# A chunked-attention and feed-forward kernel: ranked copies and splits, weight loads one pair ahead, row turns one group later, residual rows in tiles of their own

## The chip, the cores and the metric

The kernel runs on one core of a Trainium2 chip. A core has TensorE (PE in the profile, with its weight loads as PEld), VectorE (DVE), ScalarE (ACT), GpSimd (POOL) and SyncE (SP, which here only issues DMAs). Each engine works through its own queue in order. The metric is the time of one execution on the device in microseconds (us).

## The reference

Three steps follow one another, all in float32 (weights come as 64-bit numbers). B = 8, H = 8, S = 576, D = 64, so there are 4608 tokens of width 512.

```python
# 1. attention inside chunks of 64 tokens
scores = scale * q_c @ k_c^T                      # per head and chunk, 64x64
attn = softmax(scores); x = attn @ v_c            # -> [8, 576, 512]
# 2. gated mixing
gate = sigmoid(causal depthwise conv of x with conv_w, 5 taps)
x = (gate * (x @ w_val)) @ w_out
# 3. feed-forward with a residual
xn = (x - mean) / sqrt(var + 1e-6) * g_ln
out = x + relu(xn @ w_ch1) @ w_ch2                # 512 -> 2048 -> 512
```

## The kernel before

Every large product is made from three matmuls of halves: an operand is split into a high half (a rounded copy, made by ScalarE) and a low half (the difference, made by VectorE or GpSimd). High halves are named xh, gh, hh, oh, low ones xl, gl, hl, ol; the halves of a feed-forward weight tile are both named w.

**Attention stage (0 to about 382 us).** The tokens are cut into 36 units of 128. A slot `u` transposes k and q of unit u on TensorE (L177), copies them to kT and qT on ScalarE (L178), then transposes the probabilities `pr` of unit u-2 (L219, copied to pT at L220), multiplies q by k (`sc`, L192) and pr by v (`x`, L250). VectorE takes the maximum `mx`, subtracts it (`ex`), ScalarE takes the exponential (L206), and VectorE sums (`sm`, L208), inverts and scales (`pr`, L211). Transposes of k, q and pr share two PSUM tiles with the tag "t", so a transpose waits until the copy out of the tile two before is done. From x, ScalarE makes a copy xf (L264) and the high half xh (L268), and GpSimd the low half xl (L269).

Four units make a block of 512 tokens; there are nine. For each block VectorE runs the convolution `cg` (L281, 16 instructions; ScalarE makes the first tap at L279), ScalarE takes its sigmoid (L288, which needs a table load, as the next exponential does), TensorE forms the values `psv` in four groups of 12 matmuls (L295), VectorE multiplies them by the gate (`gv`, L309), ScalarE and VectorE split that (gh L312, gl L313), and TensorE multiplies by w_out (`pso`, again L295), which ScalarE copies (`y`, L325) and writes to memory. A table `dense` says which slot gets which of these steps. The weights w_out are decoded from 64-bit (ScalarE L107, VectorE L108 to L110: `da`) and split (`oh` L115, `ol` L116) by `split_w`, in four chunks.

**First feed-forward stage (about 382 to 484 us).** The first 512 tokens go through 16 groups f: `ff1` makes psh (12 matmuls), ScalarE and VectorE its halves hh (L393) and hl (L394), `ff2` uses the group before (`acc`, 12 matmuls, L409). Beside that the weights of later groups are loaded, decoded and split (`next_ff`), and the rows of the next 1024 tokens are read in pairs, normalised (`ln_rows`: statistics on VectorE, the root `r` at L357 and the scaled rows `yr` at L366 on ScalarE) and turned (`turn_rows`: 8 transposes per pair at L374).

**Pair stage (about 484 to 1172 us).** The remaining 4096 tokens run in four rounds (`s`) of 8 pairs (`p`) of column groups through `ff_pair`, which works with sums of weights and of rows. The weight sums are made once, in round 0, by `make_pair`: it reads both decoded tiles of a pair back from memory (`raws`, L439 and L440), adds them on VectorE (L441 to L444), splits the sums (`wc`) and writes them out for later rounds. The staging tag "raw" has two tiles, and a pair takes both. In the last pair of a round `ff2_tile` adds the residual rows and writes the result: the upper four tiles from `yt`, read ahead by `load_yt`, the lower four from rows read at that point by `load_rows` (L343, a staging tag with three tiles).

**What sets the order.** TensorE's instructions stand in the order of the program in slots 0 to 6 and again from the first feed-forward stage on (`manual_schedule`). Everything else is ordered by the tile scheduler, which ranks instructions by their place in the program unless they stand in a `high_priority` block.

Of the kernel before, what the change touches and what calls it, by code (L numbers as in the profile page):

```python
# [19 lines left out]
def tile_chunk_attention_gated_mlp(ctx: ExitStack, tc: tile.TileContext, q, k, v, w_val, conv_w, w_out, g_ln, w1, w2, out):  # L20
    nc = tc.nc
# [107 lines left out]
    def split_w(nm):  # L129
        hs, ls = [], []  # L130
        for c, raw in enumerate(wv[nm]):
            hi = pD1.tile([P, DM], F32R, name=f"{nm}h{c}")
            lo = pD1.tile([P, DM], F32R, name=f"{nm}l{c}")
            split(hi, lo, raw)
            hs.append(hi)
            ls.append(lo)
        wv[nm] = (hs, ls)
# [34 lines left out]
    def transpose_in(u, src, dst, nm):  # L172
# [5 lines left out]
        nc.scalar.activation(out=t, in_=ps, func=ACTF.Copy)  # L178
        dst[u] = t
# [34 lines left out]
    def a4(u):  # L214
# [5 lines left out]
        nc.scalar.activation(out=t, in_=ps, func=ACTF.Copy)  # L220
        pT[u] = t
# [18 lines left out]
    def a5(u):  # L240
# [21 lines left out]
        for lo, hi, sh in segs:  # L262
            dst = xf[j][:, :, lo + sh:hi + sh].rearrange("p (r i) t -> p r i t", r=2)
            nc.scalar.activation(out=dst, in_=x[:, :, :, lo - a:hi - a], func=ACTF.Copy)  # L264
        for lo, hi, sh in segs:
            src = xf[j][:, :, lo + sh:hi + sh]
            dst = xh[j][:, :, lo:hi].rearrange("p (r i) t -> p r i t", r=2)
            nc.scalar.activation(out=dst, in_=x[:, :, :, lo - a:hi - a], func=ACTF.Copy)  # L268
            nc.gpsimd.tensor_tensor(out=xl[j][:, :, lo:hi], in0=src, in1=xh[j][:, :, lo:hi], op=ALU.subtract)  # L269
# [27 lines left out]
    def val(j, f):  # L297
        hs, ls = wv["v"]
# [8 lines left out]
        for lo, hi, sh in ((0, o, 0), (o, BLK, HALO)):  # L307
            if lo < hi:
                nc.vector.tensor_tensor(out=gv[:, lo:hi], in0=ps[:, lo:hi], in1=cg[:, f, lo + sh:hi + sh], op=ALU.mult)  # L309
        a = pD1.tile([P, BLK], F32R, tag=f"gh{f}", name="gh")  # L310
        b = pD1.tile([P, BLK], F32R, tag=f"gl{f}", name="gl")
        nc.scalar.activation(out=a, in_=gv, func=ACTF.Copy)  # L312
        nc.vector.tensor_tensor(out=b, in0=gv, in1=a, op=ALU.subtract)  # L313
        gh[j, f], gl[j, f] = a, b

    def proj(j, t):
        hs, ls = wv["o"]
# [7 lines left out]
        nc.scalar.activation(out=y, in_=ps, func=ACTF.Copy)  # L325
        nc.scalar.dma_start(out=y_dram[j][ts, :], in_=y)
# [99 lines left out]

    def make_pair(p):
# [7 lines left out]
        ra, rb = (stg.tile([P, 4, 2 * P], F32, tag="raw", name="raws") for _ in range(2))  # L435
# [3 lines left out]
        nc.sync.dma_start(out=ra[:, 0:2, :], in_=a_dram[2 * p].rearrange("p (c w) -> p c w", c=2))  # L439
        nc.sync.dma_start(out=ra[:, 2:4, :], in_=a_dram[2 * p + 1].rearrange("p (c w) -> p c w", c=2))  # L440
# [45 lines left out]
    def load_yt(s):  # L486
        for i in range(HB, 2 * HB):
            if i % 2 == 0:
                t = p2["yt"].tile([P, 2, DM], F32, name="yt")
            nc.sync.dma_start(out=t[:, i % 2, :], in_=rows(s, i)[0])  # L490
            yt[i] = t[:, i % 2, :]

    def ff2_tile(s, p, h, i):
# [21 lines left out]
        elif last:  # L515
            y = load_rows(s, i)
            nc.vector.tensor_tensor(out=y, in0=ps, in1=y, op=ALU.add)
            nc.sync.dma_start(out=rows(s, i)[1], in_=y)

    def ff_pair(s, p, fill):  # L520
# [6 lines left out]
        def prod(ps, k, nm, start):  # L527
# [109 lines left out]
    def prep(t):  # L637
        nonlocal xn0, yt0
        if t == 0:
# [11 lines left out]
            turn_rows(ln_rows([yt0[:, i, :] for i in range(HB)]), 0)  # L651
# [26 lines left out]
    at(0, (5, 1), lambda: split_w("o"))  # L678
# [28 lines left out]
    next_ff(NFA + 1)  # L707
    ys = {0: pair_rows(0)}
    for f in range(NF):
        ff1(0, f)  # L710
        if f in (3, 5, 7, 9):
            turn_rows(ys.pop(f - 3), f - 3)
# [7 lines left out]
        if f > 0:  # L720
            next_ff(f + NFA + 1)
        if f == NF - 4:
# [14 lines left out]
    for s in range(NS):  # L737
        for p in range(NPR):
            fill = ff_pair(s, p, fill)
            if p == 0:  # L740
                load_yt(s)
# [32 lines left out]
```

## Time and profile before

| | us |
|---|---|
| three runs | 1177.71, 1178.44 (median), 1179.29 |
| profiled execution | 1179.48 |
| its span, first to last instruction | 1177.7 |
| TensorE busy | 1112.4 (94%) |
| VectorE busy | 731.0 (62%) |
| ScalarE busy | 526.3 (45%) |
| GpSimd busy | 159.8 (14%) |

A busy share is a mean over stages. What is read in the rows below is, for each engine, when an instruction started, how long it took, how long the engine had been idle before it, and which instruction ended that idle time.

### The profile page before, as it was taken

The page shows a single profiled execution, that of the slowest core. Times are in us where ns is not written, and L with a number is a line of the kernel's source. Part 1 is how long each engine was busy: PE and PEld are TensorE (multiplying, and loading weights), DVE is VectorE, ACT ScalarE, POOL GpSimd, SP SyncE. Part 2 cuts the span into 40 slices and gives each one's busy share as a digit, 9 for nine tenths or more (in the row PEclk, how much of TensorE's full clock was granted, in tenths as well). Part 3 has the DMA queues.
Part 4 walks back from the last instruction along what each step waited for, and adds up shares of the span by engine and source line. Part 5 has one row for each costly group of instructions (what it writes and reads, how often), then busy time and mean ns, then how long its engine had stood idle before and what let it go on. Part 6 is the DMA issues. An engine that isn't in the chain of part 4 may idle for free.

```text
span 1177.7 us, 18293 instructions
## 1 busy us (share of the span) xinstructions
PE 1112.4 (94%) x7128; PEld 902.3 (77%) x7128; DVE 731.0 (62%) x1237; ACT 526.3 (45%) x972; POOL 159.8 (14%) x160
## 2 busy tenths in 40 slices
PE   6869999899999799989999999999999999999998
PEld 5747777777777687768888788888788887878876
DVE  6878898998794889644653834435734446433433
ACT  4557677676766665434452323423323323221221
POOL 2231143111210444332220000000000000000000
PEclk8979999999999899999999999999999999999999
DMA  7655676665124563534333543332623332622212
GB/s 185 176 117 130 166 191 170 172 158 128 55 65 151 169 210 105 211 129 143 126 125 108 183 138 108 121 111 72 232 90 123 110 107 90 233 78 89 84 36 80
DMA packets 168860, 155.37 MB, mean 132 GB/s; under 512 B 120622, under 2 KB 128838, under 8 KB 168774
## 3 DMA queue, kind: packets, MB, share of 16 engines
q1 hardware_dynamic: 163590, 144.76, 40.3%
q10 hardware_dynamic: 5184, 9.44, 2.1%
q8 instruction: 56, 0.92, 0.3%
q14 instruction: 30, 0.25, 0.1%
HBM read 116.41 MB, written 37.75 MB: 131 GB/s over the span
## 4 chain that ended last, share of the span: by engine, by line
PE 60%; DVE 27%; ACT 6%; issue 3%; DMA 3%; SPq 1%; POOL 1%; DVEq 0%; ACTq 0%; POOLq 0%
PE acc L507 14%; PE x L533 14%; PE psf L507 13%; PE zy L533 9%; DVE cg L281 8%; PE psv L295 3%; DVE pr L211 2%; PE pso L295 2%; DVE sm L208 2%; DVE da L109 2%; DVE da L110 2%; DVE ex L202 1%; DVE gl L313 1%; DVE mx L199 1%; DVE h L543 1%
## 5 line engine op out<-in xcount | busy, mean ns | idle before, releaser
L551 DVE TENSOR_TENSOR c<-x,c 128x512 f32<-128x512 f32 x96 | 66.2, 689 | 231.6 <-ACT c L547 176.3
L507 PE MATMUL acc<-w,h 128*128 128x512 f32 x768 | 186.4, 392 | 0.0
L507 PE MATMUL psf<-w,h 128*128 128x512 f32 x768 | 186.1, 392 | 0.0
L507 PEld LDWEIGHTS acc<-w,h 128*128 128x128 f32 x768 | 144.8, 189 | 31.4
L507 PEld LDWEIGHTS psf<-w,h 128*128 128x128 f32 x768 | 144.4, 188 | 31.2
L533 PE MATMUL x<-t,wc 128*128 128x512 f32 x576 | 146.9, 391 | 2.2 <-DVE c L551 2.2
L547 ACT ACTIVATE c<-zy 128x512 f32<-128x512 f32 x96 | 57.9, 604 | 193.8 <-PE zy L533 193.7
L533 PEld LDWEIGHTS x<-t,wc 128*128 128x128 f32 x576 | 108.1, 188 | 26.0 <-DVE c L551 3.0
L542 ACT ACTIVATE h<-c 128x512 fp32r<-128x512 f32 x96 | 60.5, 631 | 138.1 <-DVE c L551 137.6
L281 DVE SCALAR_TENSOR_TENSOR cg<-xf,cw,cg 128x516 f32<-128x516 f32 (+1 forms) x176 | 116.3, 707 | 0.8 <-ACT cg L279 0.6
L512 DVE TENSOR_TENSOR yt<-psf,yt 128x512 f32<-128x512 f32 x128 | 88.0, 690 | 23.8 <-PE psf L507 19.8
L533 PE MATMUL zy<-b,wc 128*128 128x512 f32 x384 | 98.9, 393 | 0.0
L533 PEld LDWEIGHTS zy<-b,wc 128*128 128x128 f32 x384 | 71.3, 188 | 14.5
L543 DVE SCALAR_TENSOR_TENSOR h<-c,h 128x512 fp32r<-128x512 f32 x96 | 67.7, 705 | 15.6 <-ACT h L542 15.2
L269 POOL TENSOR_TENSOR xl<-xf,xh 128x512 fp32r<-128x512 f32 (+1 forms) x40 | 50.9, 1276 | 153.4 <-ACT xh L268 153.1
L295 PE MATMUL psv<-xh,vh 128*128 128x512 f32 x144 | 60.9, 423 | 6.5 <-DVE gv L309 6.3
L295 PE MATMUL pso<-oh,gh 128*128 128x512 f32 x144 | 60.4, 419 | 6.1 <-ACT gh L312 6.1
L417 POOL TENSOR_TENSOR wc<-raws,wc 128x256 fp32r<-128x256 f32 x56 | 46.8, 856 | 111.9 <-ACT wc L416 111.7
L116 POOL TENSOR_TENSOR w<-da,w 128x512 fp32r<-128x512 f32 x32 | 46.9, 1474 | 95.9 <-ACT w L115 95.9
L295 PE MATMUL psv<-xl,vh 128*128 128x512 f32 x144 | 58.8, 408 | 0.9 <-POOL xl L269 0.9
L295 PE MATMUL pso<-oh,gl 128*128 128x512 f32 x144 | 58.1, 405 | 0.9 <-DVE gl L313 0.9
L533 PE MATMUL x<-b,wc 128*128 128x512 f32 x192 | 52.6, 410 | 6.6 <-DVE h L543 5.9
(114 smaller groups left out, 1779.1 us busy)
## 6 DMA issues: line engine op xcount, KB each, us to landing
wc<-wc SPq DMA_DIRECT2D x112, 512.0 KB, 3.2
raw<-in_moe_w_ch SPq DMA_DIRECT2D x32, 512.0 KB, 4.8
yr<-yd SPq DMA_DIRECT2D x48, 256.0 KB, 3.1
vr<-in_v SPq DMA_DIRECT2D x144, 64.0 KB, 2.7
yd<-y ACTq DMA_DIRECT2D x36, 256.0 KB, 2.5
kr<-in_k SPq DMA_DIRECT2D x64, 128.0 KB, 2.9
qr<-in_q SPq DMA_DIRECT2D x64, 128.0 KB, 2.9
out<-yt SPq DMA_DIRECT2D x20, 256.0 KB, 3.2
```

What stands on the lines that cost most here:

```text
L116: nc.gpsimd.tensor_tensor(out=lo, in0=a, in1=hi, op=ALU.subtract)
L269: nc.gpsimd.tensor_tensor(out=xl[j][:, :, lo:hi], in0=src, in1=xh[j][:, :, lo:hi], op=ALU.subtract)
L281: nc.vector.scalar_tensor_tensor(out=o, in0=x[:, f, i + lo:i + hi], scalar=cw[:, i * CT + f:i * CT + f + 1], in1=o, op0=ALU.mult, op1=ALU.add,
L295: nc.tensor.matmul(out=ps, lhsT=lt, rhs=rh, start=(i == 0), stop=(i == n - 1))
L417: eng.tensor_tensor(out=lo, in0=a, in1=hi, op=ALU.subtract)
L507: nc.tensor.matmul(out=ps, lhsT=lt, rhs=rh, start=(g == 0 and k == 0 and (first or half)), stop=(g == 1 and k == 2 and (last or half)),)
L512: nc.vector.tensor_tensor(out=yt[i], in0=ps, in1=yt[i], op=ALU.add)
L533: nc.tensor.matmul(out=ps, lhsT=lt, rhs=rh, start=(start and c == 0 and i == 0), stop=(c == 1 and i == 2), skip_group_check=True)
L542: nc.scalar.activation(out=t[:, 0, :], in_=src, func=ACTF.Relu)
L543: nc.vector.scalar_tensor_tensor(out=t[:, 1, :], in0=src, scalar=0.0, in1=t[:, 0, :], op0=ALU.max, op1=ALU.subtract)
L547: nc.scalar.activation(out=t, in_=zy, func=ACTF.Copy)
L551: nc.vector.tensor_tensor(out=t, in0=x, in1=t, op=ALU.add)
```

## The change

Six edits in one diff. Copies and splits in the attention stage (kT, qT, pT, xf, xh, xl, gv, gh, gl, y and its write) and the row statistics of the first block move into `high_priority` blocks. `split_w` takes a range of chunks, and w_out's four chunks are placed in slots 5, 6, 7 and 8 instead of all in slot 5. The weights of group 5 are asked for inside the loop, behind the first pair of rows. `turn_rows` is called in groups 4, 6, 8 and 10 instead of 3, 5, 7 and 9. The loads of `make_pair` become `load_pair`, called one pair ahead. `load_yt` reads the lower four residual tiles too, in the last pair of a round, into the staging tag "raw".

```diff
-    def split_w(nm):
-        hs, ls = [], []
-        for c, raw in enumerate(wv[nm]):
+    def split_w(nm, c0=0, c1=CT):
+        hs, ls = wv.setdefault(nm + "s", ([], []))
+        for c, raw in list(enumerate(wv[nm]))[c0:c1]:
...
-        nc.scalar.activation(out=t, in_=ps, func=ACTF.Copy)
-        dst[u] = t
+        with tc.high_priority():
+            nc.scalar.activation(out=t, in_=ps, func=ACTF.Copy)
+            dst[u] = t
...
-        nc.scalar.activation(out=t, in_=ps, func=ACTF.Copy)
-        pT[u] = t
+        with tc.high_priority():
+            nc.scalar.activation(out=t, in_=ps, func=ACTF.Copy)
+            pT[u] = t
...
-        for lo, hi, sh in segs:
-            dst = xf[j][:, :, lo + sh:hi + sh].rearrange("p (r i) t -> p r i t", r=2)
-            nc.scalar.activation(out=dst, in_=x[:, :, :, lo - a:hi - a], func=ACTF.Copy)
...
+        with tc.high_priority():
+            for lo, hi, sh in segs:
+                dst = xf[j][:, :, lo + sh:hi + sh].rearrange("p (r i) t -> p r i t", r=2)
+                nc.scalar.activation(out=dst, in_=x[:, :, :, lo - a:hi - a], func=ACTF.Copy)
...
+        with tc.high_priority():
+            for lo, hi, sh in ((0, o, 0), (o, BLK, HALO)):
+                if lo < hi:
+                    nc.vector.tensor_tensor(out=gv[:, lo:hi], in0=ps[:, lo:hi], in1=cg[:, f, lo + sh:hi + sh], op=ALU.mult)
+            a = pD1.tile([P, BLK], F32R, tag=f"gh{f}", name="gh")
+            b = pD1.tile([P, BLK], F32R, tag=f"gl{f}", name="gl")
+            nc.scalar.activation(out=a, in_=gv, func=ACTF.Copy)
+            nc.vector.tensor_tensor(out=b, in0=gv, in1=a, op=ALU.subtract)
...
-        nc.scalar.activation(out=y, in_=ps, func=ACTF.Copy)
-        nc.scalar.dma_start(out=y_dram[j][ts, :], in_=y)
+        with tc.high_priority():
+            nc.scalar.activation(out=y, in_=ps, func=ACTF.Copy)
+            nc.scalar.dma_start(out=y_dram[j][ts, :], in_=y)
...
+    raws = {}
+
+    def load_pair(p):
+        ra, rb = (stg.tile([P, 4, 2 * P], F32, tag="raw", name="raws") for _ in range(2))
+        for f in range(2):
+            nc.sync.dma_start(out=ra[:, 2 * f:2 * f + 2, :], in_=a_dram[2 * p + f].rearrange("p (c w) -> p c w", c=2))
+        raws[p] = ra, rb
...
-        ra, rb = (stg.tile([P, 4, 2 * P], F32, tag="raw", name="raws") for _ in range(2))
+        ra, rb = raws.pop(p)
...
-    def load_yt(s):
-        for i in range(HB, 2 * HB):
+    def load_yt(s, half):
+        for i in range(half * HB, (half + 1) * HB):
             if i % 2 == 0:
-                t = p2["yt"].tile([P, 2, DM], F32, name="yt")
+                t = p2["yt"].tile([P, 2, DM], F32, name="yt") if half else stg.tile([P, 2, DM], F32, tag="raw", name="yt")
...
-            y = load_rows(s, i)
+            y = yt[i]
...
                 make_pair(p + 1)
+                if p + 2 < NPR:
+                    load_pair(p + 2)
...
-            turn_rows(ln_rows([yt0[:, i, :] for i in range(HB)]), 0)
+            with tc.high_priority():
+                ln_rows([yt0[:, i, :] for i in range(HB)])
+            turn_rows([yt0[:, i, :] for i in range(HB)], 0)
...
-    at(0, (5, 1), lambda: split_w("o"))
+    for c in range(CT):
+        at(0, (5 + c, 1), lambda c=c: split_w("o", c, c + 1))
...
-    next_ff(NFA + 1)
     ys = {0: pair_rows(0)}
     for f in range(NF):
         ff1(0, f)
-        if f in (3, 5, 7, 9):
-            turn_rows(ys.pop(f - 3), f - 3)
+        if f in (4, 6, 8, 10):
+            turn_rows(ys.pop(f - 4), f - 4)
...
-        if f > 0:
-            next_ff(f + NFA + 1)
+        next_ff(f + NFA + 1)
...
+    load_pair(0)
     make_pair(0)
+    load_pair(1)
...
             if p == 0:
-                load_yt(s)
+                load_yt(s, 1)
+            if p == NPR - 1:
+                load_yt(s, 0)
```

What that does to the queues is shown at three places. The first is ScalarE's queue around the sigmoid of block 0 (oh is a split chunk of w_out, ex an exponential, ACT_TABLE_LOAD and the cg behind it the sigmoid). Before:

```order
L178 ACTIVATE kT<-pst 128x512
L115 ACTIVATE oh_762<-da 128x512
L178 ACTIVATE qT<-pst 128x512
L220 ACTIVATE pT<-pst 128x512
L115 ACTIVATE oh_771<-da 128x512
L264 ACTIVATE xf<-x 128x4x128
L268 ACTIVATE xh<-x 128x4x128
L206 ACTIVATE ex_144<-ex_144 128x8x64
L288 ACT_TABLE_LOAD
L288 ACTIVATE cg<-cg 128x4x512
L178 ACTIVATE kT<-pst 128x512
L178 ACTIVATE qT<-pst 128x512
```

And with the change:

```order
L178 ACTIVATE kT<-pst 128x512
L290 ACT_TABLE_LOAD
L290 ACTIVATE cg<-cg 128x4x512
L178 ACTIVATE qT<-pst 128x512
L221 ACTIVATE pT<-pst 128x512
L115 ACTIVATE oh_859<-da 128x512
L315 ACTIVATE gh<-gv 128x512 x2
L115 ACTIVATE oh_991<-da 128x512
L266 ACTIVATE xf<-x 128x4x128
L178 ACTIVATE kT<-pst 128x512
L270 ACTIVATE xh<-x 128x4x128
L178 ACTIVATE qT<-pst 128x512
```

Table load and sigmoid now stand between the first kT and its qT, where they stood behind the exponential of that unit; two of w_out's chunks stand above the second qT and the last one (not shown) just below it. In both the second kT is behind the sigmoid.

The second place is ScalarE's queue in the first feed-forward stage, where the first pair of rows is normalised (r is the root, yr the scaled rows, hh the high half of a group, here of groups 2 and 3; da and w belong to the weights). Before:

```order
L115 ACTIVATE w_4935<-da 128x512
L393 ACTIVATE hh<-psh 128x512
L357 ACTIVATE r<-ve 128x2
L107 ACTIVATE da<-raw_5078 128x512
L357 ACTIVATE r<-ve 128x2
L115 ACTIVATE w_4944<-da 128x512
L107 ACTIVATE da<-raw_5171 128x512
L393 ACTIVATE hh<-psh 128x512
L366 ACTIVATE yr<-yr,w,r 128x512 x2
L115 ACTIVATE w_5082<-da 128x512
L366 ACTIVATE yr<-yr,w,r 128x512 x2
L107 ACTIVATE da<-raw_5080 128x512
```

And with the change:

```order
L115 ACTIVATE w_5155<-da 128x512
L361 ACT_TABLE_LOAD
L361 ACTIVATE r<-ve 128x2
L397 ACTIVATE hh<-psh 128x512
L115 ACTIVATE w_4955<-da 128x512
L107 ACTIVATE da<-raw_4953 128x512
L107 ACTIVATE da<-raw_5153 128x512
L361 ACTIVATE r<-ve 128x2
L115 ACTIVATE w_4964<-da 128x512
L370 ACTIVATE yr<-yr,w,r 128x512 x2
L397 ACTIVATE hh<-psh 128x512
L370 ACTIVATE yr<-yr,w,r 128x512 x2
```

The root has moved from behind hh of group 2 to ahead of it, with a table load of its own, and the first two scaled rows from behind hh of group 3 to ahead of it. On TensorE the 8 transposes of each pair stand one group later.

The third place is SyncE's queue at the second and third pair of the pair stage (raws is the load of a pair's decoded weights, wc a written weight sum). Before:

```order
L439 DMA raws<-ad_89 128x512
L440 DMA raws<-ad_90 128x512
L449 DMA wc_106<-wc 128x1024
L449 DMA wc_109<-wc 128x1024
L413 DMA out<-yt_4577 128x512 x4
L490 DMA yt<-yd_133 128x512 x4
L449 DMA wc_107<-wc 128x1024
L449 DMA wc_108<-wc 128x1024
L439 DMA raws<-ad_91 128x512
L440 DMA raws<-ad_92 128x512
L449 DMA wc_110<-wc 128x1024
L449 DMA wc_111<-wc 128x1024
```

And with the change:

```order
L436 DMA raws<-ad_89 128x512
L436 DMA raws<-ad_90 128x512
L459 DMA wc_106<-wc 128x1024
L459 DMA wc_109<-wc 128x1024
L417 DMA out<-yt_4577 128x512 x4
L500 DMA yt<-yd_133 128x512 x4
L459 DMA wc_107<-wc 128x1024
L459 DMA wc_108<-wc 128x1024
L436 DMA raws<-ad_91 128x512
L436 DMA raws<-ad_92 128x512
L459 DMA wc_110<-wc 128x1024
L459 DMA wc_111<-wc 128x1024
```

Apart from line numbers the rows are the same.

## Rows read from the trace of the kernel before

**Rows 1.** The page's totals: busy us of each engine, share of the span, instructions.
```profile
PE 1112.4 (94%) x7128; PEld 902.3 (77%) x7128; DVE 731.0 (62%) x1237; ACT 526.3 (45%) x972; POOL 159.8 (14%) x160
```

**Rows 2.** Busy time by stretch: length, PE, PEld, DVE, ACT, POOL, PEclk, DMA, GB/s.
```profile
385.00:480.00 95.00, 86.25 (x373) 68.96 (x373) 86.16 (x150) 57.83 (x119) 41.87 (x29) 0.96 0.48 157
600.00:1100.00 500.00, 498.60 (x2204) 406.48 (x2202) 242.18 (x399) 155.16 (x291) 6.48 (x8) 1.00 0.36 122
```

**Rows 3.** Waits of TensorE, 0 to 100 us: us in total, times, longest.
```profile
PE pst L219 <- ACT kT L178: 15.0, 6, 6.4
```

**Rows 4.** Waits of TensorE, 100 to 382 us.
```profile
PE psv L295 <- DVE gv L309: 6.3, 4, 2.8
PE pso L295 <- ACT gh L312: 6.1, 6, 2.1
PE pst L219 <- ACT kT L178: 2.0, 4, 0.6
```

**Rows 5.** TensorE in time, 56-88 us: start, duration, instruction, [idle before, releaser].
```profile
63.21 1.12 PE L219 MATMUL pst<-ident,pr 128*128 128x128 f32 x4 [4.08 <-ACT kT L178]
...
75.48 0.90 PE L219 MATMUL pst<-ident,pr 128*128 128x128 f32 x3 [6.39 <-ACT kT L178]
```

**Rows 6.** ScalarE in time, 54 to 84 us.
```profile
64.04 0.63 ACT L115 ACTIVATE oh<-da 128x512 fp32r<-128x512 f32 x1 [0.89 <-DVE da L110]
...
71.74 1.28 ACT L288 ACT_TABLE_LOAD   x1
73.04 1.91 ACT L288 ACTIVATE cg<-cg 128x2048 f32<-128x2048 f32 x1
74.85 0.58 ACT L178 ACTIVATE kT<-pst 128x512 f32<-128x512 f32 x1
```

**Rows 7.** VectorE in time, 50 to 84 us.
```profile
57.70 0.68 DVE L110 SCALAR_TENSOR_TENSOR da<-raw,da 128x512 uint32<-128x512 uint32 x1
...
70.98 0.47 DVE L281 SCALAR_TENSOR_TENSOR cg<-xf,cw,cg 128x256 f32<-128x256 f32 x1
```

**Rows 8.** Waits of VectorE, 80 to 350 us.
```profile
DVE sm L208 <- ACT ex L206: 10.7, 16, 0.9
```

**Rows 9.** All engines in time, 284 to 290 us.
```profile
286.45 1.30 POOL L269 TENSOR_TENSOR xl<-xf,xh 128x512 fp32r<-128x512 f32 x1 [6.55 <-ACT xh L268]
...
286.97 1.32 DVE L281 SCALAR_TENSOR_TENSOR cg<-xf,cw,cg 128x516 f32<-128x516 f32 x1
...
288.82 1.41 DVE L281 SCALAR_TENSOR_TENSOR cg<-xf,cw,cg 128x516 f32<-128x516 f32 x2
```

**Rows 10.** TensorE in time, 382 to 490 us.
```profile
404.89 1.97 PE L374 MATMUL pst<-ident,yr 128*128 128x128 f32 x8 [5.95 <-ACT yr L366]
...
411.24 2.96 PE L295 MATMUL psh<-xn,w 128*128 128x512 f32 x12
...
419.64 1.04 PE L374 MATMUL pst<-ident,yr 128*128 128x128 f32 x8
...
423.27 2.96 PE L295 MATMUL psh<-xn,w 128*128 128x512 f32 x12
```

**Rows 11.** All engines in time, 496 to 507 us.
```profile
496.55 1.03 SPq L439 DMA_DIRECT2D raws<-ad  x1
...
503.86 0.81 DVE L441 TENSOR_TENSOR raws<-raws 128x256 f32<-128x256 f32 x1 [4.36 <-DMA raws<-ad]
...
505.46 0.68 DVE L543 SCALAR_TENSOR_TENSOR h<-x,h 128x512 fp32r<-128x512 f32 x1
...
506.19 1.22 PE L533 MATMUL x<-b,wc 128*128 128x512 f32 x2 [5.00 <-DVE h L543]
```

**Rows 12.** VectorE in time, 1160 to 1177.7 us.
```profile
1169.51 0.69 DVE L517 TENSOR_TENSOR yr<-acc,yr 128x512 f32<-128x512 f32 x1 [0.68 <-PE acc L507]
1170.89 0.69 DVE L517 TENSOR_TENSOR yr<-acc,yr 128x512 f32<-128x512 f32 x1 [0.68 <-PE acc L507]
1173.88 0.69 DVE L517 TENSOR_TENSOR yr<-acc,yr 128x512 f32<-128x512 f32 x1 [2.30 <-DMA yr<-yd]
```

More of the change, by code (lines that the diff above doesn't have):

```diff
@@ L136, in split_w @@
             ls.append(lo)
-        wv[nm] = (hs, ls)
     w1s, w2s, wraw = {}, {}, {}
@@ L261, in a5 @@
         segs = [(max(a, lo), min(b, hi), sh) for lo, hi, sh in ((0, o, HALO), (o, BLK, 2 * HALO)) if max(a, lo) < min(b, hi)]
-        for lo, hi, sh in segs:
-            dst = xf[j][:, :, lo + sh:hi + sh].rearrange("p (r i) t -> p r i t", r=2)
-            nc.scalar.activation(out=dst, in_=x[:, :, :, lo - a:hi - a], func=ACTF.Copy)
[L265 to L269, printed above, removed]
+        with tc.high_priority():
+            for lo, hi, sh in segs:
+                dst = xf[j][:, :, lo + sh:hi + sh].rearrange("p (r i) t -> p r i t", r=2)
+                nc.scalar.activation(out=dst, in_=x[:, :, :, lo - a:hi - a], func=ACTF.Copy)
+            for lo, hi, sh in segs:
+                src = xf[j][:, :, lo + sh:hi + sh]
+                dst = xh[j][:, :, lo:hi].rearrange("p (r i) t -> p r i t", r=2)
+                nc.scalar.activation(out=dst, in_=x[:, :, :, lo - a:hi - a], func=ACTF.Copy)
+                nc.gpsimd.tensor_tensor(out=xl[j][:, :, lo:hi], in0=src, in1=xh[j][:, :, lo:hi], op=ALU.subtract)
     cg = pD1.tile([P, CT, BLK + HALO], F32, name="cg")
@@ L297, in val @@
     def val(j, f):
-        hs, ls = wv["v"]
+        hs, ls = wv["vs"]
         fs = slice(f * P, (f + 1) * P)
@@ L306, in val @@
         gv = pD2.tile([P, BLK], F32, tag="gv", name="gv")
[L307 to L313, printed above, removed]
+        with tc.high_priority():
[6 more added lines that the diff above has]
+            nc.vector.tensor_tensor(out=b, in0=gv, in1=a, op=ALU.subtract)
         gh[j, f], gl[j, f] = a, b
     def proj(j, t):
-        hs, ls = wv["o"]
+        hs, ls = wv["os"]
         ts = slice(t * P, (t + 1) * P)
@@ L438, in make_pair @@
         a21 = s1
-        nc.sync.dma_start(out=ra[:, 0:2, :], in_=a_dram[2 * p].rearrange("p (c w) -> p c w", c=2))
-        nc.sync.dma_start(out=ra[:, 2:4, :], in_=a_dram[2 * p + 1].rearrange("p (c w) -> p c w", c=2))
         nc.vector.tensor_tensor(out=s3, in0=a11, in1=a21, op=ALU.subtract)
```

## The prediction

> **What bounds the kernel now.** I read the engines' totals first, then the list of what each engine waited for, then the instructions of the stretches in which TensorE waits, and last the table of busy time by stretch. The totals [rows 1] show TensorE at 1112.4 us of a span of 1177.7, so at most 65 us can be had without taking work from it. Of these, almost nothing lies in the last and longest stage: between 600 and 1100 us TensorE is busy for 498.60 of 500 us [rows 2]. Whatever the change does there (row statistics one or two pairs earlier, residual rows in other tiles) lies beside TensorE and costs or gives nothing; if that cover is gone, a wait of ScalarE or VectorE would show as TensorE idle time behind 600 us. The waits that end on TensorE lie elsewhere: 15.0 us before 100 us on the copy kT [rows 3], 6.3 + 6.1 + 2.0 us from 100 to 382 us [rows 4]; one in the first feed-forward stage, one in the first pair and a late load at the very end are taken up with the parts that touch them.
>
> The profiled run took 1179.48 us, 1.8 more than its span and 1.0 more than the median of 1178.44. I sum against the profiled run and take the same difference off the median.
>
> The change adds no work but one table load; what it does is move instructions within their queues.
>
> **Part 1: block 0, where the splits of w_out stand.** Two stalls wait for kT, 4.08 us at 63.21 and 6.39 us at 75.48 [rows 5]. ScalarE's rows say why [rows 6]: it walks its queue in order, and at 64.04 a high half of w_out stands for 0.89 us on VectorE's decode with the copies behind it; then table load (1.28) and sigmoid (1.91) run from 71.74, and only then comes kT at 74.85. Four chunks of w_out are decoded at once; the change decodes one in each of slots 5 to 8 and ranks the copies above. ScalarE's queue then has table load and sigmoid a unit earlier, between kT and qT of the unit that stalled first. So they need the last cg a unit earlier as well. Before it starts at 70.98 on VectorE, behind all of w_out's decode, of which a chunk takes three instructions, the longer two 0.68 each [rows 7], some 1.8 in all. With two or three chunks moved behind it (3.6 to 5.4) and the four long instructions of one unit's softmax (2.7 at 0.68), the last cg comes some 6 to 8 us sooner, the sigmoid ends at about 66, qT behind it, and the second kT needs no sigmoid any more. Ceiling 4.08 + 6.39 = 10.5. I leave one wait of a sigmoid and its table load (1.91 + 1.28 = 3.2) for qT: gain 7. Ends: 0, if the last cg is no sooner and the sigmoid holds qT as long as it held kT, and 10.5.
>
> **Part 2: priority in blocks 1 to 8.** The ceiling is what TensorE waits there, 6.3 + 6.1 + 2.0 = 14.4 [rows 4]. The order helps kT and qT (in a steady block they now stand ahead of two gh) and harms the exponential: in most units it now follows xf and xh instead of standing between or before them, and each such copy takes about 0.58 (kT's 0.58 [rows 6]). VectorE already waits 10.7 us for the exponential, 16 times from 80 to 350 us [rows 8], so in 16 units the delay is paid at once: 16 x 0.58 = 9.3 at worst. What is queued behind its wait are the reciprocal and the product pr, for which TensorE's transposes wait. So the ends are 14 gained and 9 lost. I take 4 gained, a bit over a quarter of the ceiling, since the waits for gh and gv that the order addresses are 12.4 of the 14.4 and only some of the new places are ahead of them.
>
> The GpSimd subtraction xl starts earlier too. A VectorE instruction beside one: cg at 286.97 took 1.32, with xl from 286.45 to 287.75; the next two took 1.41 together [rows 9]. The Trainium skill, GPSIMD Engine Reference, section Specifications, says that GpSimd shares its SBUF interfaces with VectorE and contends with instructions that have two SBUF inputs; cg and gl are such, and by that rule a moved xl slows another neighbour instead of none; the trace agrees with the 1.32. That is in the first rival below.
>
> **Part 3: last block and the first feed-forward stage.** The square root r of the last block's rows and its table load now stand before the sigmoid: 1.28 [rows 6] lost. By the Trainium skill, ScalarE: Activation LUTs, section What ACT_TABLE_LOAD costs, a switch takes 2.66 us with its drain; here the sigmoid starts at 73.04, right behind a load from 71.74 to 73.02, so no drain is seen, and the measured 1.28 stands. By the page the sum would be 1.4 higher.
>
> The first turn of rows goes from group 3 to group 4. Its stall of 5.95 us for yr [rows 10] falls away if yr comes before the new place is due: the old one was reached at 404.89 - 5.95 = 398.9, and two groups of 12 matmuls now stand ahead, 2.96 each at most (the psh at 411.24 [rows 10]), so at 404.8. Before, yr was ready at 404.9; it now stands before hh(3) on ScalarE instead of behind it, but behind one more table load of 1.28. I expect it in time or some tenths late. With the stall goes the slow stretch behind it: from the transposes to the next psh takes 411.24 - 404.89 = 6.35, the same work later 423.27 - 419.64 = 3.63 [rows 10]: 2.7 more for the same instructions (a granted clock of 0.96 over 385 to 480 us [rows 2]: behind the stall TensorE stood at 1.2 instead of 2.4 GHz for a while). Ceiling 8.7. But what is late next is VectorE: from 385 to 480 us it is busy 86.16 of 95 us [rows 2], so it has 8.8 us to give, all of it only if it never waits. It decodes weights and makes hl, for which TensorE's second product waits. I take 5; ends 0 and 8.7. The loads of group 5's weights now stand behind those of the first rows on SyncE; that costs nothing as long as VectorE, which decodes them, is the later of the two, and else it is part of the lower end.
>
> **Part 4: weight sums a pair ahead.** The first stall of the pairs is 5.00 us at 506.19: x waits for h, which is at 505.46 on VectorE behind the weight sum at 503.86, which had waited 4.36 us for its load; that load was issued at 496.55 [rows 11]. The change moves the load in the program, but both tiles of its tag are held by the pair before until that pair is summed, and SyncE's queue holds loads and writes in the same order as before. So 0; ends: 5 gained, and 0 lost, since nothing is added there and nothing moves.
>
> **Part 5: residual rows.** The last three additions of the kernel that follow matmuls come 1.38 us apart (1169.51, 1170.89 [rows 12]); the fourth was due at 1172.27 and came at 1173.88, since its rows were loaded only when a tile came free. Now they lie ready: 1.6 gained; the output write behind it is the same. Ends: 1 and 2. The loads are now beside the last pair, where TensorE is the bound.
>
> **Sum:** -7 - 4 + 1.3 - 5 + 0 - 1.6 = -16.3; 1179.48 - 16.3 = 1163.2 on the profiled run, **1162** on the median.
>
> **Rivals.** *VectorE gives it back.* It has 8.8 us free in the first feed-forward stage and is the engine that each attention unit waits on; the moved xl slow cg instead of gl, the later exponential eats what kT gained, and hl comes no sooner. Then parts 2 and 3 are worth nothing but the lost 1.3: -7 + 1.3 - 1.6 = -7.3, 1171. For it: [rows 2, 8, 9]; against: VectorE still has idle time in both places.
>
> *The stalls go nearly whole.* 10 in block 0, 9 in the blocks, 8 in the feed-forward stage and 1.6 at the end, with the lost 1.3 hidden: -28.6, 1150. For it: these are waits for order, not for work; against: VectorE's share.
>
> *The exponential becomes the chain, and the kernel is slower.* Place: ScalarE, exp behind xf and xh in units 4 to 35; price 32 x 0.58 = 18.6 for one copy and 8 x 0.58 = 4.6 more for the second copy in units with a sigmoid, 23 in all; against it 7, 5 and 1.6 gained and 1.3 lost: +11, 1189. It decides where VectorE has no cg left to run between ex and sm. For it: the 16 waits [rows 8]; against: in the other half of the units VectorE does have such work.
>
> *It doesn't do what it says.* As the weight sums' order is unchanged, so the copies' priority may only swap who waits: the sigmoid holds qT for as long as kT was held. Then within 2 us of 1178.
>
> **How the numbers follow.** Forecast 0.50 (own range 1154 to 1168), VectorE gives it back 0.20, stalls go whole 0.13, slower 0.12, no effect 0.05. What a measurement of this kernel tells from no change is 0.2%, some 2.4 us. The first three are faster, less a little for their upper edges: faster 0.78, same 0.08, slower 0.14. The range from 1149 to 1179 leaves out most of the slower case and the tip of the best one.
>
> **What would show it.** Block 0: no kT stall above 3 us between 55 and 80 us. Blocks: TensorE's waits for gh and gv under 10 us from 100 us on; the wait of VectorE for the exponential must not grow past 15. Feed-forward: no stall at the first turn, and new short waits for hl in its place. Weight sums: the 5 us stall stays. End: fourth addition 1.4 behind the third. I am wrong if pT or qT waits replace kT's in every unit, if hl waits sum to over 6 us, or if TensorE idles behind 600 us.

## The result and the profile after

The changed kernel takes 1166.5 us, the median of four runs (1165.71 to 1167.19), against 1178.53 before in the same call: a ratio of 0.9898 [0.9881, 0.9915], so 12.0 us faster. Forecast were 1162 and a range of 1149 to 1179. Ratios leave out one disturbed run, of experiment 1's kernel (2184.3 us for some 1172), which is why that kernel was measured once more for its trace. The profiled run took 1166.13 us, its span 1164.3. The page's totals, to be held against [rows 1]:

```profile
PE 1106.6 (95%) x7128; PEld 895.1 (77%) x7128; DVE 724.2 (62%) x1237; ACT 528.0 (45%) x973; POOL 158.5 (14%) x160
```

TensorE has as many instructions and 5.8 us less busy time, which is already a hint that the same matmuls ran faster. To see where 13.4 us of span went, both traces are cut at four marks on TensorE: the first product with w_out (`pso`), the first `psh` of the feed-forward stage, the first matmul of the pair stage (`zy`), and the start of the kernel's last group of matmuls into `acc`.

| stage, us | before | after | change | forecast |
|---|---|---|---|---|
| start to first pso (block 0) | 85.75 | 78.89 | -6.9 | -7 |
| to first psh (the blocks) | 296.27 | 289.76 | -6.5 | -4 + 1.3 = -2.7 |
| to first zy (first feed-forward) | 102.56 | 104.65 | **+2.1** | **-5** |
| to the last group (pairs) | 681.99 | 681.52 | -0.5 | 0 |
| to the end | 11.13 | 9.48 | -1.6 | -1.6 |
| sum | 1177.7 | 1164.3 | -13.4 | -16.3 |

Three terms come out in size, one is too small, and of one the gain did not come. That its loss of 2.1 us is more than the difference between two traces is borne out by four others: experiments 7 and 8, which leave this stage's turns as in the change, have 104.9 and 104.7 us, experiments 1 and 4, with the turns in their old place, 102.0 and 101.8 (experiment 2, with the old turns too, has 105.2; experiment 6 comes back to that).

**Block 0.** TensorE in time, 56 to 88 us; in brackets the idle time before and what ended it. To be held against [rows 5]:

```profile
62.00 0.74 PE L219 MATMUL pst<-ident,pr 128*128 128x128 f32 x4 [3.47 <-ACT kT L178]
65.71 1.13 PE L192 MATMUL sc<-kT,qT 64*64 64x64 f32 x32 [2.96 <-ACT qT L178]
```

ScalarE in time behind it, against [rows 6]:

```profile
58.16 0.63 ACT L115 ACTIVATE oh<-da 128x512 fp32r<-128x512 f32 x1 [3.09 <-DVE da L110]
60.28 0.67 ACT L107 ACTIVATE da<-raw 128x512 f32<-128x512 f32 x1 [1.49 <-POOL ol L116]
...
61.37 0.58 ACT L178 ACTIVATE kT<-pst 128x512 f32<-128x512 f32 x1
61.97 1.28 ACT L290 ACT_TABLE_LOAD   x1
63.26 1.91 ACT L290 ACTIVATE cg<-cg 128x2048 f32<-128x2048 f32 x1
65.08 0.58 ACT L178 ACTIVATE qT<-pst 128x512 f32<-128x512 f32 x1
```

The sigmoid starts 9.8 us sooner than before (63.26 for 73.04), between kT and qT, and qT waits for it, as worked out. The first kT still waits 3.47 us. ScalarE's stand of 3.09 us on the decode ends at 58.16, before TensorE's stall begins (58.53); what holds kT is what follows: the split, 1.49 us for a staging tile that GpSimd's `ol` still reads, the copy of the next chunk at 60.28 and an exponential. How much of the 6.9 us is idle time, TensorE's busy time up to the first pso shows, before and after (length; PE, PEld, DVE, ACT, POOL; PEclk, DMA, GB/s):

```profile
0.00:85.75 85.75, 61.31 (x789) 51.52 (x789) 64.52 (x109) 47.43 (x83) 23.33 (x28) 0.86 0.65 161
```

```profile
0.00:78.89 78.89, 58.37 (x788) 49.35 (x789) 61.33 (x109) 46.96 (x83) 22.35 (x28) 0.89 0.70 173
```

TensorE is 3.9 us less idle, and 2.9 us less busy with the same matmuls (one record is missing after), at a higher mean clock.

**The blocks.** What TensorE waited for from 100 to 369 us, against [rows 4], and what VectorE waited for, against [rows 8]:

```profile
PE pso L297 <- ACT gh L315: 3.6, 6, 1.3
PE psv L297 <- DVE gv L312: 3.4, 4, 1.2
PE pso L297 <- DVE gl L316: 3.0, 3, 1.8
PE x L251 <- ACT pT L221: 2.3, 4, 0.8
PE pst L378 <- ACT yt L370: 1.6, 1, 1.6
PE pst L219 <- ACT kT L178: 0.2, 1, 0.2
```

```profile
DVE sm L208 <- ACT ex L206: 16.2, 15, 1.6
```

The waits for gh, gv and kT fell from 14.4 us to 7.2; those for gl, pT and yt (the root ahead of the last sigmoid) rose from 1.3 to 6.9. In idle time that is almost a draw (15.7 us to 14.1). Yet the stage is 6.5 us shorter. Busy time in it, same columns, before and after:

```profile
85.75:382.00 296.25, 278.37 (x2951) 222.94 (x2949) 249.11 (x426) 203.81 (x344) 53.88 (x52) 0.98 0.51 138
```

```profile
78.90:368.60 289.70, 273.64 (x2951) 219.51 (x2949) 243.31 (x426) 203.88 (x344) 54.02 (x52) 0.99 0.52 140
```

Of the 6.5 us, 278.37 - 273.64 = 4.7 are busy time of the same 2951 matmuls and only 1.8 idle time. Where the 4.7 come from is seen at one wait for gv: TensorE in time, and behind it busy time and clock of a stretch of 1.8 us, first of before:

```profile
187.71 0.50 PE L295 MATMUL psv<-xh,vh 128*128 128x512 f32 x1 [2.19 <-DVE gv L309]
...
188.76 0.63 PE L295 MATMUL psv<-xl,vh 128*128 128x512 f32 x1
...
192.17 0.39 PE L295 MATMUL psv<-xh,vh 128*128 128x512 f32 x1
```

```profile
189.00:190.80 1.80, 1.80 (x5) 1.43 (x5) 1.77 (x3) 1.80 (x5) 1.29 (x1) 0.50 0.92 255
```

and of after:

```profile
176.84 0.50 PE L297 MATMUL psv<-xh,vh 128*128 128x512 f32 x1 [1.16 <-DVE gv L312]
177.18 0.39 PE L297 MATMUL psv<-xl,vh 128*128 128x512 f32 x1
...
178.79 0.39 PE L297 MATMUL psv<-xh,vl 128*128 128x512 f32 x1
```

```profile
177.20:179.00 1.80, 1.80 (x9) 1.48 (x8) 1.80 (x4) 1.80 (x4) 0.05 (x1) 1.00 0.96 226
```

Behind the wait of 2.19 us the granted clock falls to 0.50 (1.2 GHz): eight matmuls from 188.76 to 192.17 stand 0.43 apart instead of 0.23, 1.6 us more. Behind the wait of 1.16 us it stays at 1.00. The stall of 2.19 thus cost 3.8. The stage before has four such stretches at 0.50, from about 161, 189, 226 and 373 us, 13.6 us in all; after has one, of 3.4 us from about 230. At half speed that is 6.8 and 1.7 us lost, and the 5.1 between them cover the 4.7. The length of one wait does not tell whether the clock falls: before, a wait of 2.10 us passed at 1.00, while the stretch from 161 us follows two of 1.28 and 0.52:

```profile
343.96 0.50 PE L295 MATMUL pso<-oh,gh 128*128 128x512 f32 x1 [2.10 <-ACT gh L312]
```

**The first feed-forward stage.** TensorE in time at the first turn, against [rows 10], and TensorE's waits from 375 to 520 us:

```profile
388.18 2.97 PE L297 MATMUL psh<-xn,w 128*128 128x512 f32 x12
390.98 1.03 PE L378 MATMUL pst<-ident,yr 128*128 128x128 f32 x8
```

```profile
PE acc L413 <- DVE hl L398: 7.8, 8, 1.7
PE x L543 <- DVE h L555: 3.9, 1, 3.9
PE x L543 <- DVE c L563: 2.2, 2, 1.4
PE acc L413 <- ACT hh L397: 2.1, 2, 1.1
```

The stall of 5.95 us is gone, and eight waits for hl and two for hh (9.9 us) stand in its place; before, these two came to 2.8 us in the stage. What the engines did during the stall before, and with the change in the middle of the stage and in all of it (same columns):

```profile
398.94:404.89 5.95, 0.00 (x0) 0.00 (x1) 5.79 (x20) 3.51 (x8) 1.62 (x1) 0.91 0.93 320
```

```profile
386.00:416.00 30.00, 25.30 (x115) 19.55 (x114) 28.28 (x58) 19.21 (x40) 12.43 (x8) 1.00 0.72 243
...
368.65:473.30 104.65, 94.77 (x405) 73.21 (x404) 89.25 (x151) 62.36 (x125) 43.78 (x31) 0.98 0.49 163
```

While TensorE stood, VectorE worked for 5.79 of 5.95 us. With the change it has 1.7 of 30 us idle from 386 to 416 us. Over the whole stage it is idle for 15.4, but 3.4 of them lie ahead of its first decode (one wait of 10.08 us ends at 372.08) and 6.7 behind its last, which ends at 444.0; 5.3 are left between.

**Pairs and end.** From 600 to 1100 us TensorE is busy for 498.90 of 500 us. The wait of 5.00 us [rows 11] is still there, with 3.94, and the last additions [rows 12] now stand 1.38 apart. VectorE's load wait, TensorE's wait behind it, and VectorE at the end:

```profile
491.49 0.82 DVE L451 TENSOR_TENSOR raws<-raws 128x256 f32<-128x256 f32 x1 [3.27 <-DMA raws<-ad]
```

```profile
493.83 1.65 PE L543 MATMUL x<-b,wc 128*128 128x512 f32 x3 [3.94 <-DVE h L555]
```

```profile
1159.14 0.69 DVE L527 TENSOR_TENSOR yt<-acc,yt 128x512 f32<-128x512 f32 x1 [0.68 <-PE acc L517]
1160.52 0.69 DVE L527 TENSOR_TENSOR yt<-acc,yt 128x512 f32<-128x512 f32 x1 [0.68 <-DMA out<-yt]
```

### The profile page after: what moved, and what is told of

It reads as the page before. It is cut to its first block, busy times and chain, and to the rows that moved or that the text cites. A ratio compares the mean times of both kernels' runs of the same rounds, so it can differ in the third digit from the quotient of the medians.

```text
span 1164.3 us, 18278 instructions
## 1 busy us (share of the span) xinstructions
PE 1106.6 (95%) x7128; PEld 895.1 (77%) x7128; DVE 724.2 (62%) x1237; ACT 528.0 (45%) x973; POOL 158.5 (14%) x160
## 4 chain that ended last, share of the span: by engine, by line
PE 57%; DVE 27%; ACT 6%; issue 4%; SPq 3%; DMA 2%; POOL 1%; ACTq 0%; POOLq 0%; DVEq 0%
PE acc L517 15%; PE x L543 15%; PE psf L517 14%; PE zy L543 10%; DVE cg L283 9%; DVE da L110 2%; DVE da L109 2%; DVE sm L208 2%; DVE pr L211 2%; SPq L98 1%; DVE gv L312 1%; DVE h L555 1%; SPq L89 1%; PE pst L378 1%; DVE gl L316 1%
## 5 line engine op out<-in xcount | busy, mean ns | idle before, releaser
L555 DVE SCALAR_TENSOR_TENSOR h<-c,h 128x512 fp32r<-128x512 f32 x96 | 68.2, 710 | 13.6 <-ACT h L554 13.4
```

What stands on the lines that cost most here:

```text
L555: nc.vector.scalar_tensor_tensor(out=t[:, 1, :], in0=src, scalar=0.0, in1=t[:, 0, :], op0=ALU.max, op1=ALU.subtract)
```

## The experiments

Three questions were open: whether block 0 gained by the spread of the splits or by the priority; whether the length of the first feed-forward stage is set by VectorE or by the place of the turn; and whether the weight sums' load is held by its tiles or by the order of the queue. The expectations give each theory's numbers.

Ratios are to the kernel before, run beside each. Stages that an edit doesn't touch still moved by up to some 2 us (with the turn alone, block 0 by +2.3 and the blocks by -2.2), so one stage's difference of that size between two traces proves nothing.

**1. Only the splits of w_out spread** (kernel before with this edit).

```diff
-    at(0, (5, 1), lambda: split_w("o"))
+    for c in range(CT):
+        at(0, (5 + c, 1), lambda c=c: split_w("o", c, c + 1))
```

> The kernel before with w_out's four chunks placed in slots 5 to 8 and nothing else. Theory A (the decode of w_out in one slot made block 0's stalls): first pso about 6 us earlier than 85.75, time 1172 to 1173, and nothing changes behind block 0. Theory B (the rank of the copies made block 0's gain): first pso within 1.5 us of before, time 1177 to 1179.

Measured 1171.97 (the median of three), ratio 0.9925 [0.9904, 0.9947]. The run for its trace:

> The run spread once more, for its trace. Theory A: first pso 5 to 7 us earlier than the 85.75 of the kernel before, the stretch from there to the first psh within 2 us of 296.3, the first feed-forward stage within 2 us of 102.6. Theory B: first pso within 1.5 us of before; the ratio 0.9925 measured for spread then comes from a later stage.

That run took 1170.9 us. TensorE in time in block 0:

```profile
67.16 1.12 PE L218 MATMUL pst<-ident,pr 128*128 128x128 f32 x4 [6.61 <-ACT kT L177]
```

One stall is left of two, and pso starts at 79.72, 6.0 us sooner. The blocks move by -1.4. So the spread alone brings nearly all of block 0's gain.

**2. Only the priority blocks** (kernel before with all `high_priority` blocks of the change; shown is the one for kT and qT).

```diff
-        nc.scalar.activation(out=t, in_=ps, func=ACTF.Copy)
-        dst[u] = t
+        with tc.high_priority():
+            nc.scalar.activation(out=t, in_=ps, func=ACTF.Copy)
+            dst[u] = t
...
```

> The kernel before with the high_priority blocks alone (w_out's split still all in slot 5, turns in groups 3, 5, 7, 9). Theory A: block 0 gains at most 2 us, the blocks behind it 6.5 us together, time 1170 to 1172. Theory B: block 0 gains 6 us or more and the later blocks little, first pso near 79, time about 1172 as well, so the places decide and not the sum.

Measured 1171.22, ratio 0.9922 [0.9904, 0.9940]. Block 0 gains 2.5 us (little more than untouched stages move), the blocks 8.4; the first feed-forward stage loses 2.6, with the turns in their old place. Busy time in the blocks:

```profile
83.30:371.10 287.80, 271.68 (x2950) 218.46 (x2949) 243.49 (x426) 203.16 (x344) 53.28 (x52) 1.00 0.52 140
```

TensorE's busy time is 6.7 us below that of before: here too most of the gain is clock. The priority makes the gain of the blocks, and the spread that of block 0. Together the two are not worth their sum (8.8 + 9.2 us by the ratios): with the end's 1.6 it would be 19.6, and the change has 12.0; without the later turn (experiment 4) it has 15.8.

**3. Only the turn a group later** (kernel before).

```diff
-        if f in (3, 5, 7, 9):
-            turn_rows(ys.pop(f - 3), f - 3)
+        if f in (4, 6, 8, 10):
+            turn_rows(ys.pop(f - 4), f - 4)
```

> The kernel before with the row turns one group later and group 5's weights asked for inside the loop. Theory V (the first feed-forward stage lasts as long as VectorE's decode and hl need, 86 us of work behind its first decode): the 5.95 us stall goes, waits for hl of 6 to 9 us take its place, psh to zy stays within 2 us of 102.6, time 1177 to 1180. Rival S (the stall's loss passes through and something else in the whole change took it back): psh to zy falls to 94 to 96, time about 1171.

Measured 1181.25, ratio 1.0014 [1.0000, 1.0027]: nothing gained. The stall for yr is gone here as well, and the stage takes 103.8 us instead of 102.6; TensorE waits 5.8 us for hl and 2.1 for hh. This alone contradicts the step that expected 5 us.

**4. The turn back in its old place** (changed kernel).

```diff
-        if f in (4, 6, 8, 10):
-            turn_rows(ys.pop(f - 4), f - 4)
+        if f in (3, 5, 7, 9):
+            turn_rows(ys.pop(f - 3), f - 3)
```

> The changed kernel with the row turns back in groups 3, 5, 7 and 9 (all else kept). Theory V (VectorE sets the length of the first feed-forward stage): a wait for yr of 4 to 6 us returns at the first turn and the waits for hl shrink by as much; the ratio to the kernel before stays within 0.2% of the changed kernel's 0.9898. Rival S (the later turn is worth its stall): 6 to 8 us slower than the changed kernel, ratio about 0.996.

Measured 1163.71, ratio 0.9866 [0.9851, 0.9882], some 4 us better than the change by the ratios, whose intervals just touch, and more than the 0.2% that theory V allowed. TensorE's stall is back, shorter, the waits for hl and hh fall from 9.9 to 3.9 us, and the stage is 101.8 us, 2.8 shorter than after:

```profile
388.73 1.97 PE L378 MATMUL pst<-ident,yr 128*128 128x128 f32 x8 [3.41 <-ACT yr L370]
```

```profile
368.40:470.20 101.80, 94.39 (x405) 74.85 (x404) 85.42 (x151) 61.89 (x125) 42.38 (x31) 0.97 0.51 168
```

VectorE's 151 instructions are the same as after and take 85.42 us instead of 89.25. Where the difference comes from is experiment 6's matter.

**5. Two decode instructions less** (changed kernel; leaves out the sign and the low bits of the feed-forward weights of groups 5 to 15).

```diff
         nc.vector.tensor_scalar(out=au, ... logical_shift_left)
+        if short:
+            return
         nc.vector.scalar_tensor_tensor(out=au, in0=hw, ...)
         nc.vector.scalar_tensor_tensor(out=au, in0=lw, ...)
```

> The changed kernel without the last two of the three decode instructions on VectorE for the weights of groups 5 to 15 (sign and low bits are left out): 22 halves x 1.37 = 30 us less for VectorE in the first feed-forward stage, nothing less on TensorE. Theory V: the waits for hl and hh (9.9 us) go to under 2, psh to zy falls from 104.65 to 95 to 97, ratio 0.9898 - 8/1178 = 0.983. Rival Q (hl is late because of its place in the queue behind waits for loads, not because VectorE is full): psh to zy stays above 101, ratio above 0.987.

Measured 1153.07, ratio 0.9777 [0.9760, 0.9793]. The stage:

```profile
367.40:458.60 91.20, 90.17 (x405) 73.05 (x405) 54.96 (x110) 61.64 (x125) 39.35 (x32) 1.00 0.59 202
```

With 34 us taken off VectorE the stage falls by 13.5 us, more than the 8 to 10 expected, to 1 us above TensorE's busy time at full clock. VectorE and what feeds it set the length of this stage.

**6. Low halves of the late weights on VectorE** (changed kernel).

```diff
-        nc.gpsimd.tensor_tensor(out=lo, in0=a, in1=hi, op=ALU.subtract)
+        (nc.vector if late else nc.gpsimd).tensor_tensor(out=lo, in0=a, in1=hi, op=ALU.subtract)
```

> The changed kernel with the low halves of the weights of groups 4 to 15 made on VectorE instead of GpSimd: 24 instructions more on VectorE, none of GpSimd's beside it. In the changed kernel 21 VectorE instructions of this stage took 19.5 us more than their like, each beside a GpSimd subtraction. Theory C (that is what a GpSimd subtraction costs VectorE, about 0.95 each): 24 x (0.68 - 0.95) = -6 us for VectorE, stage 2 to 5 us shorter, ratio 0.986 to 0.988. Rival W (the long ones are long for another reason): 24 x 0.68 = 16 us more on a full engine, stage 8 to 16 us longer, ratio about 1.0.

Measured 1154.56, ratio 0.9792 [0.9778, 0.9807]: as much as experiment 5, with all the work done. The engine that sets the stage got 23 instructions more and was busy for less time:

```profile
368.30:458.80 90.50, 90.06 (x406) 73.08 (x405) 83.96 (x174) 59.35 (x120) 8.29 (x6) 1.00 0.53 174
```

Why, the changed kernel's VectorE and GpSimd show in time, between 381 and 384 us (VectorE's rows first, GpSimd's below):

```profile
381.23 0.69 DVE L109 SCALAR_TENSOR_TENSOR da<-raw,da 128x512 uint32<-128x512 uint32 x1
381.96 1.67 DVE L110 SCALAR_TENSOR_TENSOR da<-raw,da 128x512 uint32<-128x512 uint32 x1
```

```profile
381.32 1.75 POOL L116 TENSOR_TENSOR w<-da,w 128x512 fp32r<-128x512 f32 x1 [3.75 <-ACT w L115]
```

and this experiment's VectorE:

```profile
372.71 0.68 DVE L110 SCALAR_TENSOR_TENSOR da<-raw,da 128x512 uint32<-128x512 uint32 x1
373.31 1.28 DVE L116 TENSOR_TENSOR w<-da,w 128x512 fp32r<-128x512 f32 x2
```

While GpSimd subtracts, the instruction on VectorE takes 1.67 instead of 0.68, about 1.0 more; the subtraction on VectorE itself costs 0.64. (The instruction at 381.23 had begun 0.09 us ahead of GpSimd's and took its usual 0.69; GpSimd's then took 1.75, where others took 1.3.)

Count as long each VectorE instruction of the stage that takes 0.3 us or more above the median of its operation and shape without a GpSimd instruction beside it. Every long one, in every trace, lies beside one of GpSimd. After, before and here all 49 of them began behind GpSimd's instruction and ended a fixed time behind its end: 0.55 us where 0.68 is usual, 0.28 where 0.42, 1.08 where 1.21, 0.02 where 0.15. So VectorE's instruction stands until GpSimd's is over, and the 1.0 is what was left of that. What they take above that median sums to 20.8 us after (23 long ones), 17.1 in experiment 4 (21), 17.6 before (20) and 2.9 here (6). That accounts for the 3.8 us of VectorE's time between after and experiment 4: other neighbours, not other work. Over the eight kernels whose decode and splits are alike, the length of the stage goes with this sum and not with the place of the turn: 17.0 to 17.6 us in the three of 101.8 to 102.6 us (before, 1, 4), 19.3 to 21.8 in the five of 103.8 to 105.2 (2, 3, after, 7, 8), of which experiment 2 has the old turn. What in the order of the instructions brings them side by side was not tested.

The gain, 14 us in the stage, is far above the 2 to 5 expected. TensorE's waits for hl and hh fall from 9.9 to 0.4 us, and its 405 or 406 matmuls take 4.7 us less busy time. Why 5.3 us less on VectorE do that much is not taken apart. That a decode's staging tile now comes free without the step on GpSimd explains little: ScalarE waited 2.3 us for it after and 0.8 here.

**7. Loads that really go ahead** (changed kernel; a pair takes one "raw" tile, the sums stand in two "da" tiles).

```diff
-        ra, rb = (stg.tile([P, 4, 2 * P], F32, tag="raw", name="raws") for _ in range(2))
+        ra = stg.tile([P, 4, 2 * P], F32, tag="raw", name="raws")
...
+        rb, rc = (stg.tile([P, 2, 2 * P], F32, tag="da", name="sums", bufs=3) for _ in range(2))
```

> The changed kernel, with the weight sums in two tiles of the row staging tag, so that the two raw tiles alternate between pairs and the next pair's loads do stand a pair earlier in SyncE's queue. Theory O (the load was late because both tiles were held): VectorE's weight sum finds its data, the 3.94 us stall of x is gone, time 1166.5 - 4 = 1162 to 1163. Rival D (the load is late because the DMA queues are full with writes and rows at that point): the stall keeps 3 us or more, time 1166 to 1167.

Measured 1169.29, ratio 0.9903 [0.9880, 0.9926]: no gain over the change. VectorE and TensorE in time:

```profile
478.62 1.00 DVE L452 TENSOR_TENSOR sums<-raws 128x256 f32<-128x256 f32 x1 [0.50 <-DMA raws<-ad]
...
487.31 0.93 DVE L455 TENSOR_TENSOR sums<-raws,sums 128x256 f32<-128x256 f32 x1 [1.98 <-POOL wc L421]
```

```profile
488.89 1.06 PE L544 MATMUL x<-t,wc 128*128 128x512 f32 x2 [4.75 <-DVE c L564]
```

The load is issued at 473.67 instead of 485.26 and comes nearly in time (a wait of 0.50 for 3.27), so it was the held tiles that kept it. But now the fourth sum waits for a sum tile that the pair before holds until GpSimd has split it, and TensorE's stall moves to c, 4.75 us. One wait took the place of the other.

**8. One sum tile less** (experiment 7, with s4 written over a12 on GpSimd after a12's split).

```diff
-        nc.vector.tensor_tensor(out=s4, in0=a12, in1=s2, op=ALU.subtract)
+            if k == 0:
+                nc.gpsimd.tensor_tensor(out=s4, in0=a12, in1=s2, op=ALU.subtract)
```

> The changed kernel, its weight-sum loads alternating between the two raw tiles, two of the sums in one tile of the row staging tag and the fourth sum on GpSimd in the place of an operand that is used up. Unlike the run raws, no sum waits for a tile that the pair before holds. Theory O: no wait for a load and none for a sum, x's stall of 3.94 us falls under 1, ratio 0.9898 - 3.5/1178 = 0.987. Rival M (the wait moves on once more, to the splits on ScalarE and GpSimd that the first pairs need): some stall of 2 to 4 us stays between zy and 510 us, ratio 0.989 to 0.991.

Measured 1162.09, ratio 0.9853 [0.9834, 0.9872], about 5 us better than the change. TensorE:

```profile
486.53 0.73 PE L545 MATMUL x<-t,wc 128*128 128x512 f32 x2 [2.66 <-DVE c L565]
```

From the first zy to the last group it takes 676.3 us instead of 681.5; of these 5.2 us half are waits and half busy time of the same matmuls. A wait of the size that rival M named stays, but the time is below what either theory gave.

**9. A better version: 6 and 8 together.** Then, as two more kernels, this with all weight splits' low halves on VectorE (bestv), and this with xl on VectorE instead (bestx).

```diff
-                nc.gpsimd.tensor_tensor(out=xl[j][:, :, lo:hi], in0=src, in1=xh[j][:, :, lo:hi], op=ALU.subtract)
+                nc.vector.tensor_tensor(out=xl[j][:, :, lo:hi], in0=src, in1=xh[j][:, :, lo:hi], op=ALU.subtract)
```

> dvelo and raws4 together on the changed kernel. If their gains lie in different stages they add: 0.9792 + 0.9853 - 0.9898 = 0.9747, stage psh to zy 90 to 91, no x stall over 3 us behind it. If the pairs' sums are now asked for earlier than the splits can make them, raws4 adds nothing and the ratio stays near 0.979.

> best with the low halves of all other weights (w_val, w_out, groups 0 to 3, all in the attention stage) on VectorE too: 16 instructions more there, 16 of GpSimd's less beside it. By a cost of 0.95 for a GpSimd subtraction against 0.68 for one of its own VectorE gains 4 us at most, 1 to 3 in the time; if VectorE's wait for the high half (in order, a ScalarE instruction) costs more than that, 1 to 4 us slower than best.

> best with the 40 low halves xl of the attention stage on VectorE. By the same price 40 x (0.68 - 0.95) = -11 us of VectorE's work, of which 2 to 5 reach the time, since TensorE is the bound in most of each block; if not every xl lies beside a VectorE instruction with two inputs (32.5 us idle VectorE time beside some), the 27 us more of own work make it 2 to 8 us slower than best.

Measured 1148.08, ratio 0.9731 [0.9699, 0.9764]; 1143.59, 0.9700 [0.9674, 0.9726]; and 1142.31, 0.9687 [0.9661, 0.9713]: each beats both kernels, and the gains of 6 and 8 add up (0.0106 + 0.0045 off 0.9898 would be 0.9747). VectorE's convolution cg, by line, count, busy us and mean ns, in best and in bestx:

```profile
L283 DVE SCALAR_TENSOR_TENSOR cg<-xf,cw,cg 128x516 f32<-128x516 f32 (+1 forms) x176 | 118.5, 713 | 0.4
```

```profile
L283 DVE SCALAR_TENSOR_TENSOR cg<-xf,cw,cg 128x516 f32<-128x516 f32 (+1 forms) x176 | 109.0, 659 | 0.4
```

VectorE takes over xl and pays a part of it out of faster cg. But up to the first psh it is busy 5.8 us longer than in best (310.25 for 304.45), where 11 less were expected, and still that stretch is 7.2 us shorter; how is not taken apart. The times of bestv and bestx overlap, so which is faster is open, and the two together were not run.

## Why the prediction came out as it did

**Block 0, 7: right in size (6.9), in part by luck.** The mechanism is there: the spread decode lets the last cg and the sigmoid come earlier (experiment 1: 6.0 of the 6.9), the second kT stall is gone, and qT waits 2.96 us of the 3.2 left to it. But the sum took the first kT stall as gone too, and 3.47 of its 4.08 us stayed, past the test "no kT stall above 3 us". Idle time fell by 3.9 us only; the other 2.9 are faster matmuls, which the sum had left out.

**The blocks, 4 gained less 1.3: too small, measured 6.5.** The mechanism held on both sides. TensorE's waits fell by 3.2 us for the 4 forecast, and the root's table load cost 1.6 (the wait for yt) for 1.3. The wait of VectorE for the exponential grew past the 15 us named (16.2), but no waits of TensorE for pr came of it. The mis-sized term is the ceiling of 14.4: it counted the waits alone and left out the slow matmuls that follow some of them; the busy time gained is 4.7 of the 6.5. The prediction had priced just this stretch at the first turn of rows (2.7), and not here. The rival "the exponential becomes the chain" fell: the waits came, the price did not.

**First feed-forward, 5 gained: wrong, measured a loss of 2.1.** The step that failed is "it has 8.8 us to give ... I take 5". VectorE's idle time was taken as a reserve anywhere in the stage. Two thirds of it lie ahead of the first decode and behind the last; in the middle VectorE is busy for 28.28 of 30 us, and a stall of TensorE there is time in which VectorE catches up (5.79 of the 5.95 us before). Take the stall away and TensorE waits for hl instead: 7.8 us, past the 6 named as proof of error. Experiments 3 (turn alone: 1.0014), 4 (turn undone: better) and 5 (VectorE relieved: 13.5 us) show it from three sides. So of the rival "VectorE gives it back" this part is true; on the blocks it is half true, since longer waits for gl and pT took back 4.0 of the 7.2 us that shorter ones gave. What the prediction did not see is the second half: GpSimd's subtractions make VectorE's load depend on who is beside whom. The Trainium skill, GPSIMD Engine Reference, section Specifications, names the contention, for VectorE instructions in a 2-port perf mode or with two SBUF inputs; the traces agree and give it a size, about 1.0 us more for one of 0.68. Instructions with one tensor input were held too (L108 at 394.19 took 1.52 us, its like 0.42); whether those run in such a mode, no run here shows. The prediction weighed this rule for xl alone, not for the weight splits of this stage, where GpSimd has 31 instructions and experiment 6 left 6. That the change's loss of 2.1 us comes from there is borne out by the sums of experiment 6, but no run changed the neighbours alone.

**Weight sums, 0: right** (-0.5), and for the reason given: experiment 7 shows that the held tiles kept the load. That freeing them would bring 5 us was the upper end; it took experiment 8 to get there, since the sums' own tile was late next.

**End, 1.6: right** to a tenth. **Pairs, 0: right.** The whole came within 4.5 us because the blocks gave 3.8 us more and the feed-forward stage 7.1 less than forecast, so the nearness of the total is in part luck; and the range, up to 1179, would have held no change (1178.5) as well.

## What to carry to other kernels

Before a stall is priced, ask which engine catches up during it: idle time of that engine counts only where it lies beside the stall, so read its busy share in stretches of that place and not over the stage. A wait on TensorE costs its length and, behind some, slow matmuls, which the busy time of the same instructions in two traces shows. And before work is moved to GpSimd to relieve VectorE, compare VectorE's like instructions with and without a neighbour there.

## What the hardware showed that was not expected

A GpSimd subtraction of 128x512 (1.3 to 1.75 us) held up a VectorE instruction of 0.68 us that began behind it until it was over, for about 1.0 us, more than the 0.64 us that VectorE takes for the subtraction: so giving VectorE 23 more of them made it less busy (89.25 to 83.96 us). Instructions of 0.15 and 0.42 us were held as well (up to 1.27 and 1.52). And matmuls behind a wait of 2.19 us stood 0.43 apart for 3.4 us, at a granted clock of 0.50, while those behind a wait of 1.16 us went on at 1.00, but so did those behind one of 2.10 us.
